# A list-scheduled attention and feed-forward kernel: landings as measured, and new positions and engines for its jobs

## The chip, the cores and the metric

One Trainium2 chip, one of its cores. The metric is device time in microseconds (us), the median of runs. PE is TensorE (PEld its weight loads), DVE is VectorE, ACT is ScalarE, POOL is GpSimd and SP is SyncE, which here only starts transfers.

## The reference, cut to what matters

```python
k_proj = einsum('ks,bhsd->bhkd', E, k)          # 8 batches, 8 heads, 1024 tokens, 64 wide; k = 64
v_proj = einsum('ks,bhsd->bhkd', F, v)
scores = q @ k_proj.T / sqrt(64)                # 1024 x 64 per head
scores = scores - max(scores)                   # along the 64
attn   = exp(scores);  attn = attn / (sum(attn) + 1e-9)
x      = (attn @ v_proj) as 8192 tokens x 512
out    = (sigmoid(x @ w_gate) * (x @ w_val)) @ w_out      # 512 -> 1536 -> 512
```

## The kernel before, in words

**Work.** Each batch's tokens are taken as two blocks of 512, each from two halves (`hf` 0 and 1) of q; there are 16 blocks. Attention makes x for a batch, transposed, in `xT` (two buffers, by batch). Heads go in two groups of four, R = 0 and 1. For a block, three quads, each a third of the hidden width for gate and for value, are made by a scheme of seven products of half blocks (`seven`, `product`) in place of eight: it needs sums of weights (`tG`, `tV`, from `w_sum`, L557), sums of x (`xS`, from `xs_sum`, L557; the first, S1, is A21 + A22) and copies and sums of results (L542 on ACT, L1156 on DVE). The gate is a tanh on ACT (L542), its product with the value is L1225 on DVE. The output products (`o_jobs`) use sums of hidden values (`hS`, POOL and DVE, L557) and of wO (L1259). Block 0 and the outputs of block 0 and the last block are made plainly: `plain_steps` (L1044), 12 slices of 128 columns, eight matmuls of 512 columns each, and L1066 on DVE.

**Batch 0** (`first_batch`, `FB`) is made by PE transposes, not by transfers: k is projected (`project0`), scaled and copied (`kpd`, L914 on DVE or L542 on ACT), turned (`kpD`, L886), q is turned (`qT`, L752 on DVE or L542), then scores, row maxima (L1645), subtraction (L1672 on DVE, or a matmul with `minus` and `top` on PE), exponential (L542), row sums (L989, L990), normalisation (L996 on DVE or POOL, into `wT`, which holds nothing else yet), a turn into `eT`, the product with v (`h_xo`), copies into `xT` (L886 or L542). For the other batches the turns are transposing transfers that SP issues (L1493 for q, L1687 for the exponentials, L1751 for x), and the loads of a batch are issued by POOL (L569) once x of the batch before has been turned.

**Order.** No order is written by hand. Every piece of work is a job with an engine, a position, a cost and a release time. The `Scheduler` goes through time: each engine, when free, takes the ready job with the lowest position, if its buffers are to be had (8 PSUM banks, 13 buffers) and its position lies within `window` of PE's first open job. The result is each engine's fixed order; on the chip each waits on semaphores in that order. Positions are numbers in `AT` (all batches) and `FB` (batch 0); names with `f_` in `FB`, and `s0` to `s7`, `x1` to `x4`, `g1` to `g4`, `d0` to `d2` in `AT` choose an engine. `x1=1` puts the sum S1 of every block from 2 on (`x_sums`) on POOL. `EXTRA` adds time to jobs of a name: short visits of PE between longer products had such additions (`sc0`, `sc`, `xo`). `K_AT`, `Q_AT`, `V_AT` and `LAND` are the release times of jobs that read loads of batch 0 and of weights; `busy0` says from when each engine is free (for POOL, the end of its issue of the loads). Where PE has nothing ready before a time `warm`, it takes a filler: two matmuls of 128 columns of the identity into bank 7 (`busy(2)`), which keeps that bank until then.

**Loads.** E and F from SP; all else from POOL, in the order k (four quarters) with the first half of q, v, wG and wV parts 0 (two halves), 3 and 1, the second half of q, parts 4, 2 and 5. This start is not scheduled (`start_loads`); wO and batch 1's loads are jobs.

Of the kernel before, what the change touches and what calls it, by code (L numbers as in the profile page):

```python
# [21 lines left out]


AT = dict(
    window=39.691, step=0.195, lag=0.031, ostep=0.461, tanh=24.746, hidden=-7.261, oa=0.642, ob=4.537,
    sums=0.006, late=-2.968, sc=2.958, scs=0.019, out=-6.538, outs=0.319, loads=18.861, gap=0.015, kv=10.106,
    tq=0.36, xa=0.682, xb=19.738, kv1=-4.582, vv1=11.125, wo=9.153, f_wo=0, qt1=-10.965, sc1=8.783,
    scs1=0.553, late1=-8.564, out1=-6.359, outs1=0.013, osum=18.731, loads2=-2.786, tq2=15.696, kv2=5.021,
    xa2=2.02, xb2=5.69, o0=8.301, o0s=1.088, xs1=-1.514, sc2=-4.038, end=3.656, pesub=8.049, s0=0, s1=0, s2=0,
    s3=0, s4=0, s5=0, s6=0, s7=0, o0p=1, o1p=0, o2p=0, o3p=1, x1=0, x2=0, x3=0, x4=0, g1=0, g2=0, g3=0, g4=1,  # L30
    d0=1, d1=0, d2=1, dsub=-4.028, dexp=-11.886, dinv=-7.839, ddiv=-2.87, dplus=-7.33, dsnap=7.354,
    dmerge=-9.93, dcopy=0.06, dturn=1.147, pdma=0.652, pact=0.017, pdve=0.019, ppool=0.074, lag0=1.549,
    lag1=1.843, lag2=-0.006, lag3=0.662, lag4=0.576, lag5=-0.336,
)
FB = dict(
    pk0=7.446, pk1=-8.728, tk0=5.506, tk1=4.235, tq00=13.818, tq01=0.999, sc00=-4.241, sc01=-3.946,
    tp00=1.262, tp01=6.936, pv0=-1.685, pv1=6.136, xo00=-7.862, xo01=-9.679, tq10=-22.633, tq11=3.073,
    sc10=-0.964, sc11=-4.904, tp10=0.8, tp11=-10.391, xo10=15.714, xo11=-2.829, wq0=15.106, wq1=11.887,
    wq2=19.985, dsum=-12.859, dnorm=10.025, m0=1.346, m1=8.435, m2=-10.899, m3=-4.159, m4=15.774, m5=5.879,
    ms=9.909, xs0=-16.282, ld1=19.781, lda=-7.826, f_pk00=1, f_pk01=0, f_pk10=1, f_pk11=0, f_tk0=1, f_tk1=1,  # L40
    f_pv00=1, f_pv01=0, f_pv10=0, f_pv11=0, f_s00=0, f_s01=1, f_s10=0, f_s11=1, f_n00=1, f_n01=0, f_n10=0,
    f_n11=0, f_tq000=1, f_tq001=1, f_tq010=0, f_tq011=1, f_tq100=0, f_tq101=1, f_tq110=1, f_tq111=1,
    f_tp000=1, f_tp001=0, f_tp010=1, f_tp011=1, f_tp100=0, f_tp101=1, f_tp110=0, f_tp111=0, f_xo000=1,
    f_xo001=0, f_xo010=0, f_xo011=1, f_xo100=1, f_xo101=1, f_xo110=0, f_xo111=1, f_dp=0, f_dx=1, f_dq=1,
    f_dk=0, f_w2=1, f_late=0, f_q1=0, f_q2=0, f_wsG0=0, f_wsG1=1, f_wsG2=0, f_wsV0=0, f_wsV1=0, f_wsV2=0,
    f_xs0=0, f_xs1=0, tx10=-12.089, tx11=4.878, f_tx100=1, f_tx101=0, f_tx110=1, f_tx111=0, late0=-10.759,
    f_ou100=0, f_ou101=0, f_ou102=0, f_ou103=0, f_ou110=0, f_ou111=1, f_ou112=1, f_ou113=1,
)


# [110 lines left out]
class Scheduler:  # L161
# [2 lines left out]
    HOP = {"PE": 0.205, "ACT": 0.035, "DVE": 0.035, "POOL": 0.06, "SP": 0.1}  # L164

    EXTRA = dict(
        qt=0.12, qt1=0.16, turnk=0.1, turnk0=0.1, tp=0.1, tx=0.1, tk=0.1, tq=0.1, bc0=0.8, den0=0.2, sc0=0.15, xo0=0.2, sc=0.03, xo=0.04,
        copyG=0.028, copyV=0.028, copyO=0.028, tanh=0.015, kd=0.1, vd=0.1,
    )

# [13 lines left out]
    def job(self, eng, pos, body, release=0.0, name=""):  # L184
        j = Job(eng, pos, body, release, name)
        self.jobs.append(j)
        self.now = j
        body()
        j.cost += self.EXTRA.get(name, 0.0)
        self.now = None  # L190
        return j
# [194 lines left out]
def bass_linformer_attn__then__ffn_glu_sigmoid_kernel(  # L386
# [20 lines left out]
    with contextlib.ExitStack() as es:  # L407
# [9 lines left out]
        def within(shape, dtype):  # L417
# [52 lines left out]
        NB = 11  # L470
# [3 lines left out]
        bank = [  # L474
            es.enter_context(nc.psum_tensor(n, [P, 512], FP32))
            for n in ("pF0", "pF1", "pF2", "pF3", "pA0", "pA1", "pA2", "pA3")
        ]

        plan = Plan()
        busy0 = {"PE": 8.3, "ACT": 8.4, "DVE": 7.0, "POOL": 18.3, "SP": 8.3}  # L480
        sched = Scheduler(range(8), range(2 + NB), 8.3, AT["window"], 38.0, busy0, 21.0)
        sched.free["bank"][7] = 21.2

        def add(eng, fn, r=(), w=(), x=(), dma=None, cost=0.0, nbytes=0, port=False):
            if sched.now is not None:
# [23 lines left out]
        def new_group():  # L509
            group[0] = []  # L510
# [212 lines left out]
        def busy(n):  # L723
            for _ in range(n):
                mm(7, bank[7][:, 0:P], ident[:, :], ident[:, :], ["ident"], n=P)
# [54 lines left out]
        def h_xo_keep(hf, R, g, bk, eng):  # L780
            o = xT[0][:, hf, g, 2 * R : 2 * R + 2, :]
            i = PB(bk)[:, :].rearrange("p (x c) -> p x c", x=2)
            copy(eng, o, i, [], [("xTt", 0, 2 * hf + g, R)], bk, 512)


        def first_batch():
            K_AT, Q_AT = ((9.15, 10.45), (13.0, 14.3)), ((11.75, 15.6), (30.05, 31.4))
            V_AT = ((18.2, 18.2), (19.5, 20.75))
            ENGS = ("ACT", "DVE", "POOL")

            def step(name, key, n, body, keep, release=0.0):
                new_group()
                b = new_bank(dirty=True)
                p = FB[f"{name}{key}"] + 0.003 * n
                bodies = body if isinstance(body, list) else [body]
                rel = release if isinstance(release, tuple) else (release,)
                for f, at_ in zip(bodies, rel):
                    job("PE", p, lambda f=f: f(b), release=at_, name=name)
                for m, f in enumerate(keep):
                    eng = ENGS[FB[f"f_{name}{key}" + ("" if name == "tk" else str(n * len(keep) + m))]]  # L800
                    job(eng, p, lambda f=f, eng=eng: f(b, eng), name=name + "k")
# [21 lines left out]
            for hf in range(2):  # L823
# [39 lines left out]
                for R in range(2):  # L863
                    if not hf:
                        keep = [lambda b, eng, R=R, g=g: keep_v0(R, b, g, eng) for g in range(2)]
                        step("pv", R, 0, [lambda b, R=R, th=th: project_v0(R, b, th) for th in range(2)], keep, V_AT[R])
                    new_group()
# [3 lines left out]
                    for g in range(2):  # L871
                        eng = ENGS[FB[f"f_xo{hf}{R}{g}"]]
                        job(eng, p, lambda R=R, g=g, hf=hf, b=bb[g], eng=eng: h_xo_keep(hf, R, g, b, eng), name="xok")
            for _ in range(120):
                j = Job("PE", 9e9, lambda: busy(2), 0.0, "fill")
                sched.now = j
                busy(2)
                sched.now = None
                j.deps = {}
                sched.fillers.append(j)  # L880
# [36 lines left out]
        def project_v0(R, bk, th):  # L917
            src = KV[1][:, :, :].rearrange("p h (t d) -> p t h d", t=NT)
            for t in range(4 * th, 4 * th + 4):
                for g in range(2):  # L920
                    mm(
                        bk,
                        PB(bk)[64 * g : 64 * g + 64, 0:256],
                        EFT[:, t, 64:128],
                        src[:, t, 4 * R : 4 * R + 4, :],
                        [("KVp", 1, R, th), ("KV", 1, R), ("EFT", t // 4)],
                        start=(t == 0),
                        stop=(t == NT - 1),
                        tp=(0, 64 * g),
                        n=256,  # L930
                        conc=2,
                        fill=0.005 + 0.094 * (t % 4 == 0 and g == 0),
                    )

        def keep_v0(R, bk, g, eng):
            gg, hh = slice(64 * g, 64 * g + 64), slice(4 * R, 4 * R + 4)
            i = PB(bk)[gg, 0:256].rearrange("p (h d) -> p h d", h=4)
            copy(eng, vpD[0][gg, hh, g, 0:DH], i, [], [("vpD", 0, g, R)], bk, 270 if eng == "ACT" else 380)
# [71 lines left out]
        def send_p0(t):  # L1010
# [8 lines left out]
            )  # L1019

        LAND = {
            "G": (21.3, 22.7, 27.4, 35.4, 24.7, 32.8, 38.1),
            "V": (22.0, 23.4, 28.7, 36.7, 26.0, 34.1, 39.4),
        }

        def landed(n, j):
# [767 lines left out]
        def load_o():  # L1794
# [7 lines left out]
            )  # L1802

        first_batch()
        plain_steps()
        for i, f in enumerate((lambda R: load_kv(0, k, 1, R), lambda R: load_q(1, R), lambda R: load_kv(1, v, 1, R))):
# [108 lines left out]
```

## Time and profile before

| | us |
|---|---|
| median of 3 runs | 525.74 (525.73 to 525.82) |
| the profiled execution | 525.35 |
| its span, first to last instruction | 523.6 |
| mean granted TensorE clock | 0.997 |
| first matmul / first plain matmul / first quad of block 2 | 5.54 / 27.09 / 99.61 |
| PE busy from 100 to 500 us | 399.97 |

Busy shares of the span: PE 97%, DVE 87%, ACT 71%, POOL 28%. A busy PE is one with matmuls in flight. Times in the timeline are the start and the length of a run of like instructions; the lengths of pipelined instructions overlap, so that costs are taken from start to start. Transfers started by POOL are short as instructions; their landing comes 5 to 30 us later and is read from the part on transfers.

### The profile page before, as it was taken

To read this page: it belongs to the slowest core of one execution; us is meant where nothing else is said; L and a number is where in the kernel's file an instruction comes from. 1 tells how busy PE (TensorE), PEld (TensorE's weight loads), DVE (VectorE), ACT (ScalarE), POOL (GpSimd) and SP (SyncE) were. 2 spreads that over 40 slices of the span, in tenths; PEclk is the share of its full clock that TensorE was granted. 3 is DMA by queue.
4 is the path that set the end of the run, shared out by engine and by line. 5 is a ranking of instruction groups with operands and counts; after the bars stand their busy time and mean duration, and the time that the engine had idled before them with its cause. 6 is when DMAs were issued, how large, how long until landed. Compare 5 with 4: busy or idle time off the path is not lost.

```text
span 523.6 us, 12301 instructions
## 1 busy us (share of the span) xinstructions
PE 510.3 (97%) x4787; PEld 428.8 (82%) x4792; DVE 457.3 (87%) x867; ACT 371.2 (71%) x711; POOL 147.5 (28%) x180
## 2 busy tenths in 40 slices
PE   5799999999999999999999999999999999999997
PEld 5544786888888888888888888888888888888885
DVE  5789999688999889997999889998899979998770
ACT  2335776688867788667976789667987679667852
POOL 9930002520336022520236003350225102420110
PEclk9989999999999999999999999999999999999999
DMA  9999914899378955599277983889557992632004
GB/s 163 197 199 207 181 41 92 213 181 161 70 173 129 223 80 107 135 192 227 40 114 158 212 146 62 182 140 223 82 102 132 200 213 42 139 63 81 3 1 162
DMA packets 140522, 71.59 MB, mean 137 GB/s; under 512 B 97200, under 2 KB 132272, under 8 KB 140464
## 3 DMA queue, kind: packets, MB, share of 16 engines
q0 software_dynamic: 35904, 29.89, 37.2%
q1 hardware_dynamic: 104560, 40.91, 37.0%
q8 instruction: 38, 0.62, 0.5%
q14 instruction: 20, 0.16, 0.1%
HBM read 60.29 MB, written 16.78 MB: 147 GB/s over the span
## 4 chain that ended last, share of the span: by engine, by line
PE 93%; DVE 4%; DMA 1%; ACT 0%; issue 0%; POOL 0%; SPq 0%; DVEq 0%
PE pA L528 47%; PE pF L528 46%; DVE hT L1066 1%; DMA EF<-in_F_dram 1%; DVE wT L996 1%; DVE inv L989 0%; DVE top L1645 0%; ACT spare L542 0%; DVE xT L886 0%; DVE wG L557 0%; DVE topf L1645 0%; POOL wT L996 0%; DVE tV L557 0%; DVE inv L990 0%; DVE pA L1672 0%
## 5 line engine op out<-in xcount | busy, mean ns | idle before, releaser
L542 ACT ACTIVATE spare<-pF 128x512 f32<-128x512 f32 (+2 forms) x164 | 92.4, 581 | 36.4 <-PE pF L528 30.6
L557 POOL TENSOR_TENSOR hT<-hT,hS 128x512 bf16<-128x512 bf16 x42 | 49.1, 1188 | 243.5 <-PE pA L528 141.8
L542 ACT ACTIVATE spare<-pA 128x512 f32<-128x512 f32 (+2 forms) x153 | 87.8, 584 | 32.8 <-PE pA L528 23.0
L1734 POOL TENSOR_TENSOR KVs<-spare,inv 128x384 bf16<-128x384 f32 (+1 forms) x51 | 37.0, 731 | 77.8 <-ACT spare L542 66.3
L542 ACT ACTIVATE spare<-spare 128x512 f32<-128x512 f32 x74 | 46.8, 637 | 4.6 <-DVE spare L1156 4.4
L1156 DVE TENSOR_TENSOR spare<-pA,spare 128x512 f32<-128x512 f32 x59 | 39.7, 677 | 7.6 <-ACT spare L542 4.5
L528 PE MATMUL pA<-wO,hT 128*128 128x256 bf16 (+1 forms) x334 | 45.6, 280 | 0.1
L1156 DVE TENSOR_TENSOR spare<-pF,spare 128x512 f32<-128x512 f32 x52 | 35.4, 682 | 9.4 <-ACT spare L542 5.6
L1225 DVE SCALAR_TENSOR_TENSOR hT<-spare,pF 128x512 bf16<-128x512 f32 x63 | 42.6, 677 | 0.5
L528 PE MATMUL pF<-wO,hT 128*128 128x256 bf16 (+1 forms) x273 | 41.4, 295 | 0.2
L1225 DVE SCALAR_TENSOR_TENSOR hT<-spare,pA 128x512 bf16<-128x512 f32 x51 | 34.4, 678 | 3.8 <-PE pA L528 2.9
L528 PEld LDWEIGHTS pA<-wO,hT 128*128 128x128 bf16 x336 | 32.5, 98 | 6.2
L528 PE MATMUL pF<-xT,wV 128*128 128x256 bf16 (+1 forms) x220 | 35.0, 282 | 0.0
L528 PE MATMUL pF<-xT,wG 128*128 128x256 bf16 (+1 forms) x208 | 34.6, 289 | 0.3 <-DVE xT L886 0.2
L528 PEld LDWEIGHTS pF<-wO,hT 128*128 128x128 bf16 x276 | 26.5, 98 | 8.5
L528 PE MATMUL pA<-xT,wV 128*128 128x256 bf16 (+1 forms) x188 | 32.0, 291 | 1.0 <-ACT spare L542 1.0
L528 PE MATMUL pA<-xT,wG 128*128 128x256 bf16 (+1 forms) x200 | 32.4, 284 | 0.0
L528 PE MATMUL pF<-xS,tV 128*128 128x256 bf16 x208 | 31.2, 272 | 0.0
L528 PE MATMUL pA<-xS,wG 128*128 128x256 bf16 x192 | 28.9, 273 | 0.0
L528 PE MATMUL pA<-xS,tG 128*128 128x256 bf16 x184 | 27.6, 273 | 0.0
L528 PE MATMUL pF<-xS,wV 128*128 128x256 bf16 x184 | 27.4, 273 | 0.0
L528 PE MATMUL pF<-xS,tG 128*128 128x256 bf16 x176 | 26.4, 273 | 0.0
(169 smaller groups left out, 1291.1 us busy)
## 6 DMA issues: line engine op xcount, KB each, us to landing
out_dram<-ost SPq DMA_DIRECT2D x63, 256.0 KB, 2.5
KVs<-in_v_dram POOLq DMA_DIRECT2D x15, 512.0 KB, 10.3
KVs<-in_k_dram POOLq DMA_DIRECT2D x14, 512.0 KB, 7.7
Qb<-in_q_dram POOLq DMA_DIRECT2D x14, 512.0 KB, 16.0
wO<-in_moe_w_out_dram POOLq DMA_DIRECT2D x1, 1536.0 KB, 26.1
wG<-in_moe_w_gate_dram POOLq DMA_DIRECT2D x5, 256.0 KB, 16.1
wV<-in_moe_w_val_dram POOLq DMA_DIRECT2D x5, 256.0 KB, 16.9
KVs<-in_k_dram POOLq DMA_DIRECT2D x4, 256.0 KB, 6.6
```

The lines of the kernel that those rows point to most:

```text
L528: lambda e: e.matmul(o, lhsT, rhs, **kw),
L542: lambda e: e.activation(o, i, func, scale=scale),
L557: fn = lambda e: e.tensor_tensor(o, a, b, op)
L996: fn = lambda e: e.tensor_tensor(o, x, i, ALU.mult)
L1066: lambda e: e.scalar_tensor_tensor(hT[0][:, m, :], BF(sg), 1.0, PB(bv)[:, :], ALU.add, ALU.mult),
L1156: lambda e: e.tensor_tensor(PB(b)[:, :] if stay else BF(s), PB(b)[:, :], BF(s), ALU.add),
L1225: lambda e: e.scalar_tensor_tensor(o, y.rearrange("p (j c) -> p j c", j=2), 1.0, x.rearrange("p (j c) -> p j c", j=2), ALU.add, ALU.mult,),
L1734: fn = lambda e: e.tensor_tensor(xto.rearrange("p (g h d) -> p h g d", g=2, h=H)[:, hh[0] : hh[1], :, :], o[:, :, 0:DH].rearrange("p (h g) ...
```

## The change

It replaces the numbers of `AT` and `FB` and the planner's assumptions; no function's work changes. The cut below has all of the latter, and the engine choices that move work.

```diff
 AT = dict(
-    window=39.691, step=0.195, ..., sc=2.958, ..., out=-6.538, ..., xa=0.682, xb=19.738, ..., wo=9.153, ...
-    ..., sc2=-4.038, end=3.656, ..., x1=0, ..., pdma=0.652, pact=0.017, pdve=0.019, ppool=0.074, ...
+    window=43.429, step=0.213, ..., sc=0.426, ..., out=-9.903, ..., xa=6.379, xb=25.171, ..., wo=20.6, ...
+    ..., sc2=-4.115, end=3.543, ..., x1=1, ..., pdma=0.759, pact=0.021, pdve=0.026, ppool=0.053, ...
 FB = dict(
-    ..., f_pk01=0, f_tk1=1, f_pv00=1, f_s00=0, f_s10=0, f_s11=1, f_n00=1, f_n11=0, f_wsG1=1, f_wsV0=0, ...
+    ..., f_pk01=1, f_tk1=0, f_pv00=0, f_s00=1, f_s10=1, f_s11=0, f_n00=0, f_n11=1, f_wsG1=0, f_wsV0=1, ...
@@ Scheduler
-        qt=0.12, ..., bc0=0.8, den0=0.2, sc0=0.15, xo0=0.2, sc=0.03, xo=0.04,
+        qt=0.12, ..., bc0=0.8, den0=0.2, xo0=0.2,
@@
-        busy0 = {"PE": 8.3, "ACT": 8.4, "DVE": 7.0, "POOL": 18.3, "SP": 8.3}
-        sched = Scheduler(range(8), range(2 + NB), 8.3, AT["window"], 38.0, busy0, 21.0)
-        sched.free["bank"][7] = 21.2
+        busy0 = {"PE": 7.35, "ACT": 8.2, "DVE": 7.7, "POOL": 19.7, "SP": 7.35}
+        sched = Scheduler(range(8), range(2 + NB), 7.35, AT["window"], 37.0, busy0, 25.0)
+        sched.free["bank"][7] = 25.2
@@ first_batch
-            K_AT, Q_AT = ((9.15, 10.45), (13.0, 14.3)), ((11.75, 15.6), (30.05, 31.4))
-            V_AT = ((18.2, 18.2), (19.5, 20.75))
+            K_AT, Q_AT = ((7.3, 8.5), (11.1, 12.45)), ((9.8, 13.85), (29.0, 30.3))
+            V_AT = ((16.35, 16.35), (18.4, 19.6))
@@
-            for _ in range(120):
+            for _ in range(170):
@@
-            "G": (21.3, 22.7, 27.4, 35.4, 24.7, 32.8, 38.1),
-            "V": (22.0, 23.4, 28.7, 36.7, 26.0, 34.1, 39.4),
+            "G": (20.3, 21.6, 26.3, 34.4, 23.65, 31.65, 37.1),
+            "V": (20.95, 22.35, 27.65, 35.75, 25.0, 33.15, 38.45),
```

What the built programs show of it: PE starts on k's first quarter right behind the transposes of E and F (16 fillers stood between); batch 0's first half has its subtractions on PE for both head groups (one before) and its normalisations on DVE (two of four were on POOL); POOL issues batch 1's v ahead of wO and the second half of its k behind q; S1 of 14 blocks is on POOL, that of blocks 2 and 3 ahead of batch 2's loads; the four weight sums on POOL are those of wV's first third (wG's second before). The number of fillers used falls from 96 to 86 matmuls.

More of the change, by code (lines that the diff above doesn't have):

```diff
@@ L24 @@
 AT = dict(
[L25 to L33, printed above, removed]
+    window=43.429, step=0.213, lag=0.011, ostep=0.464, tanh=21.597, hidden=-6.907, oa=0.549, ob=4.538,
+    sums=0.447, late=-1.505, sc=0.426, scs=0.02, out=-9.903, outs=0.016, loads=18.806, gap=0.012, kv=10.052,
@@ new lines @@
+    tq=0.487, xa=6.379, xb=25.171, kv1=-0.479, vv1=16.37, wo=20.6, f_wo=1, qt1=10.731, sc1=6.703, scs1=0.023,
+    late1=-8.42, out1=-5.011, outs1=0.053, osum=20.656, loads2=4.118, tq2=11.749, kv2=4.432, xa2=9.481,
+    xb2=-6.344, o0=6.554, o0s=0.102, xs1=-1.114, sc2=-4.115, end=3.543, pesub=13.162, s0=0, s1=0, s2=0, s3=0,
+    s4=0, s5=0, s6=0, s7=0, o0p=1, o1p=0, o2p=0, o3p=1, x1=1, x2=0, x3=0, x4=0, g1=0, g2=0, g3=0, g4=1, d0=1,
+    d1=0, d2=1, dsub=-5.317, dexp=-17.482, dinv=-6.2, ddiv=-5.811, dplus=-3.25, dsnap=6.491, dmerge=-11.783,
@@ L34 @@
+    dcopy=2.796, dturn=-1.745, pdma=0.759, pact=0.021, pdve=0.026, ppool=0.053, lag0=1.3, lag1=1.293,
+    lag2=-1.302, lag3=0.509, lag4=0.756, lag5=-0.457,
 )
 FB = dict(
[L36 to L44, printed above, removed]
@@ L45 @@
-    f_dk=0, f_w2=1, f_late=0, f_q1=0, f_q2=0, f_wsG0=0, f_wsG1=1, f_wsG2=0, f_wsV0=0, f_wsV1=0, f_wsV2=0,
-    f_xs0=0, f_xs1=0, tx10=-12.089, tx11=4.878, f_tx100=1, f_tx101=0, f_tx110=1, f_tx111=0, late0=-10.759,
-    f_ou100=0, f_ou101=0, f_ou102=0, f_ou103=0, f_ou110=0, f_ou111=1, f_ou112=1, f_ou113=1,
+    pk0=15.403, pk1=-16.99, tk0=8.488, tk1=-14.934, tq00=7.381, tq01=-9.651, sc00=-9.907, sc01=-24.495,
+    tp00=12.189, tp01=-0.744, pv0=9.411, pv1=-5.578, xo00=1.333, xo01=-16.402, tq10=-6.727, tq11=6.953,
@@ new lines @@
+    sc10=-9.441, sc11=-11.644, tp10=10.439, tp11=10.864, xo10=8.058, xo11=-10.078, wq0=13.384, wq1=9.184,
+    wq2=20.207, dsum=-20.382, dnorm=7.126, m0=-13.283, m1=8.591, m2=-17.12, m3=-4.892, m4=7.653, m5=17.37,
+    ms=4.645, xs0=-3.154, ld1=27.986, lda=-2.593, f_pk00=1, f_pk01=1, f_pk10=1, f_pk11=0, f_tk0=1, f_tk1=0,
+    f_pv00=0, f_pv01=0, f_pv10=0, f_pv11=0, f_s00=1, f_s01=1, f_s10=1, f_s11=0, f_n00=0, f_n01=0, f_n10=0,
+    f_n11=1, f_tq000=1, f_tq001=1, f_tq010=0, f_tq011=1, f_tq100=0, f_tq101=0, f_tq110=1, f_tq111=0,
@@ new lines @@
+    f_tp000=0, f_tp001=0, f_tp010=1, f_tp011=0, f_tp100=1, f_tp101=1, f_tp110=0, f_tp111=0, f_xo000=1,
+    f_xo001=0, f_xo010=0, f_xo011=1, f_xo100=1, f_xo101=0, f_xo110=0, f_xo111=0, f_dp=0, f_dx=1, f_dq=1,
+    f_dk=0, f_w2=1, f_late=0, f_q1=0, f_q2=0, f_wsG0=0, f_wsG1=0, f_wsG2=0, f_wsV0=1, f_wsV1=0, f_wsV2=0,
+    f_xs0=0, f_xs1=0, tx10=-21.46, tx11=-4.012, f_tx100=1, f_tx101=0, f_tx110=1, f_tx111=0, late0=-9.502,
+    f_ou100=0, f_ou101=1, f_ou102=0, f_ou103=0, f_ou110=1, f_ou111=1, f_ou112=0, f_ou113=0,
@@ L166 @@
     EXTRA = dict(
-        qt=0.12, qt1=0.16, turnk=0.1, turnk0=0.1, tp=0.1, tx=0.1, tk=0.1, tq=0.1, bc0=0.8, den0=0.2, sc0=0.15, xo0=0.2, sc=0.03, xo=0.04,
+        qt=0.12, qt1=0.16, turnk=0.1, turnk0=0.1, tp=0.1, tx=0.1, tk=0.1, tq=0.1, bc0=0.8, den0=0.2, xo0=0.2,
         copyG=0.028, copyV=0.028, copyO=0.028, tanh=0.015, kd=0.1, vd=0.1,
```

## The prediction

> **What bounds the kernel now.** I read the page's busy shares first, then the windows, the chain of waits, the timeline by engine and the landings of the loads.
>
> The page's first part says that TensorE is the bound:
>
> ```profile
> PE 510.3 (97%) x4787; PEld 428.8 (82%) x4792; DVE 457.3 (87%) x867; ACT 371.2 (71%) x711; POOL 147.5 (28%) x180
> ```
>
> PE lacks 13.3 us of the span of 523.6: 5.54 before its first matmul, 2.7 after its last, 5.05 between. The windows (us; then busy time of PE, PEld, DVE, ACT, POOL; granted clock; DMA share; GB/s) place the last part:
>
> ```profile
> 20.00:22.00 2.00, 0.47 (x8) 0.20 (x4) 1.01 (x2) 0.00 (x0) 1.87 (x2) 1.00 1.45 195
> ...
> 27.00:31.00 4.00, 3.96 (x20) 1.25 (x20) 3.00 (x9) 0.60 (x1) 0.00 (x0) 0.66 1.46 200
> ...
> 100.00:200.00 100.00, 99.97 (x956) 87.22 (x955) 91.02 (x165) 80.81 (x154) 25.34 (x29) 1.00 0.80 149
> ```
>
> The reader is to see that from 100 us on nothing can be won, and that the head loses in two ways: PE stands (20 to 22 us), and runs at a reduced clock (0.66 on average in 27 to 31 us, 0.50 in its worst slices). The chain of waits from 19 us (start, us, what) says why:
>
> ```profile
> 19.72 1.30 DVE top L1645 x2
> ...
> 21.06 1.05 POOL wT L996
> ...
> 22.15 0.40 PE pF L528 x4
> ...
> 24.35 0.66 DVE inv L989
> ...
> 27.09 1.01 PE pF L528 x2
> ```
>
> The normalisation `wT<-EF,inv` stands on GpSimd at 21.06, behind the issue of all weight loads (the last, wO, is issued at 19.72 and takes 1.21). Its sums were ready at 18.15 and 18.94. The last line is the first matmul of the plain blocks. And earlier PE spends time on fillers while data are there:
>
> ```profile
> 7.28 1.91 PE L528 MATMUL pA<-ident 128*128 128x128 bf16 x16
> 9.12 0.67 PE L528 MATMUL pF<-KVs,EFT 128*64 128x256 bf16 x8
> ```
>
> k's first quarter is issued at 1.37 and takes 5.5 to land, so 6.9; the matmuls that read it start at 9.12, behind 16 fillers.
>
> **What stays.** Counted by form, the two programs' PE instructions differ in fillers (96, then 86) and in subtractions on PE (4, then 6 of 512 columns, 0.22 each; both more lie before the first plain matmul). With start-to-start times of the timeline (0.216 us for 512 columns, 0.109 for 256, 0.056 for 128) the work from the first plain matmul to the first quad of block 2 is 68.9 us in both. Before, it took 99.61 - 27.09 = 72.5: the half clock cost 1.3 (27.09 to 30.50 holds work for 2.1), PE stood for 1.6 in all (0.99 at 37.6 us), 0.7 is small gaps. So the time is: start of the plain matmuls, plus fixed work, plus stalls.
>
> **What costs nothing by itself.** The landings, GpSimd's free time, the filler allowance (170) and the dropped allowances for short visits are figures of the plan: no load starts earlier by them, and no instruction takes longer. They act through the order alone, which I read from the built program.
>
> **The head, step by step.** The first 25 loads keep their order on GpSimd's queue, so I take their landings from the trace: q 9.6 and 13.6, k's last quarter 12.3, v 16.2, 18.2 and 19.4, wG part 0 at 20.05 and 21.45, wV part 0 at 20.75 and 22.15, part 3 at 23.45 and 24.8, q's second half 28.75 and 30.1, part 4 to 33.0, part 2 to 35.5.
> - k starts at 7.4 when the transposes of E and F end. Scores need k's copies (2 x 0.4), q (9.6), a transpose and a copy (0.4 each): 11.6 where they were at 13.64.
> - Row maxima to 13.1; two subtractions on PE (0.22) in place of two on DVE (0.60); exponentials (0.55) to 14.55; sums and normalisation on DVE (0.8 + 0.6) to 16.3 and 18.0, where GpSimd gave 22.1 and 23.95.
> - v at 16.2, then ACT's queue: four copies and two exponentials from 17.3 to 20.15. First product at 20.2, its copies to 21.7.
> - First plain matmul: 21.8. The weights would allow 20.8. **-5.3 us** (20.8 to 24.5: a few hand-offs 0.2 later each).
> - Behind it: second halves wait 0.55 for an xT copy that queues on DVE behind a weight sum waiting for wG part 3 (23.45), and part 2 costs 0.2: 0.75 of stalls for 1.6, **-0.85**.
> - Fillers run on to 22 us, so the half clock should go: **-1.3** (0 to -1.3).
>
> As the rows stand, the clock fell though PE never stood for more than 1.7 us in a row. [...]
>
> Outside this path, GpSimd gives up the four weight sums of one third of wG for those of wV and two early normalisations for two late ones; before, it stood idle from 40 to 53 us, so it can hold them. Its first q load then goes out near 29.5 (33.79 before), since the sums ahead of it wait for wV part 3 (24.8) and take 3 x 1.2.
>
> First quad of block 2: 92.2 instead of 99.6, **-7.45**. The covers hold: block 1 has its k by 61.5 (same bytes in the queue; PE wants it at 62.8); wO lands some 5.3 later, behind v (2 x 2.66), at 51, when DVE reaches its first sum at about 52; DVE's queue from the first row maximum (31) to block 2's sums adds up to 55.5, so 87 for 92.
>
> **What is late next.** Batch 2. Its chain before:
>
> ```profile
> 103.50 1.55 POOL L569 DMA_DIRECT2D KVs<-in_k_dram x2 [4.59 <-DMA xT<-KVs]
> ...
> 144.69 6.00 SPq L1751 DMA_TRANSPOSE xT<-KVs  x3
> ...
> 152.85 0.60 PE L528 MATMUL pF<-xT,wG 128*128 128x256 bf16 x4
> ```
>
> Loads start when batch 1's last transpose lands; xT is ready near 150; PE uses it at 152.85, nearly 3 us of slack. After the change PE is 7.45 earlier, but the loads only some 5.6: x sum 1 now stands on GpSimd in front of them (1.19 by the row of its like, L557 on POOL), and the last xT transpose queues on SP behind the output stores. And PE's order has the products of token tile 1 just before the quads: at 143.0, then copy 0.5, division 0.8, GpSimd's next 0.6, SP 1.3 and about 2 to land: 149.1. PE reaches the quads at 146.9. **+2.2** (0 to 4.5). Later batches have 8 us between products and quads. The rest of the body: 0 to 2, by its 0.13 us of idle before; I take **+0.3**. The tail has the same steps: 0.
>
> **Sum** against the profiled execution: -5.3 - 0.85 - 1.3 + 2.2 + 0.3 = -4.95; span 518.65, its own time 525.35 becomes 520.4. The median of the runs is 0.39 above it: **520.8**.
>
> **Rivals.**
> 1. The whole head gain stays (batch 2 finds its xT in time): 525.74 - 7.5 = 518.2. For it: transposes land 3.2 us after issue at the median, and the loads may start earlier. Against: the order above. Chance 0.20.
> 2. The head gives half: ACT's chain of six steps slips, or the clock halves again as PE waits at 20 to 24 us. First plain matmul at 24, clock unchanged: -3.1 - 0.85 + 1 (smaller wait at batch 2) = -3, 522.8; with the whole wait 524. Chance 0.17.
> 3. **Slower.** The first x sum of 14 blocks goes from DVE (0.41) to GpSimd (1.19). The two engines get in each other's way:
>
> ```profile
> 34.41 1.61 DVE L557 TENSOR_TENSOR wG<-wG 128x512 bf16<-128x512 bf16 x1
> 34.55 1.17 POOL L557 TENSOR_TENSOR tG<-wG 128x512 bf16<-128x512 bf16 x1
> ```
>
> 1.61 in place of 0.41, for one GpSimd sum beside it. DVE is 91% busy in the body. If each of 14 sums cost PE 0.85, that is 11.9: 525.74 - 4.95 + 11.9 = 532.7. It decides from 4.95/14 = 0.35 us a block. [...] Against the rival: xT of later batches lands some 8 us before the sum's first reader, and DVE loses 14 x 0.34 of work. Chance 0.08.
> 4. It does nothing that can be measured (within 0.2%, about what a measurement here tells from no change): landings are the plan's figures alone and move no load. But PE's order does change, and DVE takes over GpSimd's normalisation. Chance 0.05.
>
> The forecast has the other 0.50. Faster: 0.50 + 0.20 + 0.16 = 0.86; same 0.05; slower 0.09. The range for 8 in 10 leaves out rival 3 and the outer parts of 1 and 2: 517.6 to 524.4.
>
> **What would show it.** First plain matmul (`xT,wG` 128x512) at 21.8; clock 1.0 in 25 to 30 us; no PE idle at 20 to 22; first quad of block 2 at about 92; a PE wait for the xT transposes near 147 to 149; no PE wait for POOL's xS after 160. Wrong, if the plain matmuls start after 25, if PE waits more than 5 us at batch 2, or if PE's idle after 160 us passes 2.

## The result, and the profile after

The changed kernel takes **529.68 us** (median of 4 runs, 528.95 to 530.42) against 525.74 beside it; the ratio is 1.0081 with a 95% interval of 1.0058 to 1.0104. It is slower by 0.8%. The prediction was 520.8 with a range to 524.4.

The profiled run took 528.95, its span is 527.2. The page's first part (busy time of each engine):

```profile
PE 513.4 (97%) x4784; PEld 427.8 (81%) x4784; DVE 448.3 (85%) x845; ACT 374.6 (71%) x717; POOL 166.0 (31%) x194
```

PE is busy 3.1 us longer for nearly the same work (it has 10 fillers less and two subtractions more). The windows shown of before have the head mended now and the body broken:

```profile
20.00:22.00 2.00, 2.00 (x36) 1.40 (x32) 1.93 (x5) 1.95 (x5) 0.74 (x2) 1.00 1.44 194
27.00:31.00 4.00, 4.00 (x26) 2.07 (x25) 2.91 (x5) 1.91 (x5) 1.56 (x2) 1.00 1.45 196
100.00:200.00 100.00, 95.79 (x885) 80.83 (x883) 86.84 (x152) 74.03 (x141) 28.55 (x32) 0.98 0.75 135
```

PE no longer stands in 20 to 22 us and its clock is full in 27 to 31; but between 100 and 200 us, where it had lost 0.03 us, it stands for 4.2, and the mean clock there is 0.98. PE's timeline gives the stages:

```profile
23.52 0.59 PE L528 MATMUL pF<-xT,wG 128*128 128x512 bf16 x2
...
94.66 0.60 PE L528 MATMUL pF<-xT,wG 128*128 128x256 bf16 x4
...
157.10 0.60 PE L528 MATMUL pF<-xT,wG 128*128 128x256 bf16 x4
...
184.31 1.92 PE L528 MATMUL pA<-KVs,EFT 128*64 128x512 bf16 x16
```

These are the first plain matmul, the first quad of block 2, the first quad of block 4 (the first to read x of batch 2), and the projection of batch 3's k and v. At the second and the fourth the PE work still to come is the same in both programs, so they cut the time into stages that can be compared; the third is not such a mark (2 us of PE work have changed sides). Before, they were at 27.09, 99.61, 152.85 and 181.76. So the head gains 4.95, the stretch from 94.66 to 184.31 takes 89.65 in place of 82.15 and **loses 7.5**, and the rest loses 1.05: -4.95 + 7.5 + 1.05 = +3.6, which is 528.95 - 525.35.

Where the 7.5 lie, by windows of ten (columns as above: PE, PEld, DVE, ACT, POOL, clock, DMA), first in before:

```profile
120.00:130.00 10.00, 10.00 (x95) 8.45 (x92) 7.88 (x13) 8.56 (x16) 0.00 (x0) 1.00 0.95 165
130.00:140.00 10.00, 9.97 (x105) 8.47 (x103) 10.00 (x18) 8.53 (x17) 3.38 (x3) 1.00 0.28 54
140.00:150.00 10.00, 10.00 (x107) 9.03 (x106) 9.90 (x27) 9.46 (x21) 4.53 (x6) 1.00 0.63 108
150.00:160.00 10.00, 10.00 (x95) 8.92 (x93) 9.95 (x19) 5.61 (x12) 4.42 (x5) 1.00 0.56 159
```

then in the changed kernel:

```profile
120.00:130.00 10.00, 10.00 (x96) 8.98 (x95) 6.26 (x10) 8.72 (x17) 3.37 (x3) 1.00 0.56 110
130.00:140.00 10.00, 9.24 (x99) 8.01 (x97) 7.44 (x13) 8.49 (x18) 0.00 (x0) 1.00 0.25 48
140.00:150.00 10.00, 8.68 (x78) 6.99 (x78) 10.00 (x23) 5.09 (x10) 2.19 (x3) 1.00 0.78 150
150.00:160.00 10.00, 7.96 (x61) 5.92 (x62) 10.00 (x20) 4.85 (x10) 8.02 (x10) 0.83 0.59 121
```

DVE is idle for 6.3 us in the first 20 and then full for 20; PE stands for 4.1 in the 40, and its clock falls. A full DVE alone does not explain that: in before it is as full from 130 to 160 us, and PE does not stand. DVE's timeline says what it waited for in its idle time, the scores of batch 2 (idle time before, in brackets):

```profile
127.57 0.69 DVE L1645 TENSOR_REDUCE topf<-pA 128x8 f32<-128x512 f32 x1 [2.01 <-PE pA L528]
...
131.07 0.69 DVE L1645 TENSOR_REDUCE topf<-pA 128x8 f32<-128x512 f32 x1 [1.60 <-PE pA L528]
...
133.91 0.69 DVE L1645 TENSOR_REDUCE topf<-pA 128x8 f32<-128x512 f32 x1 [1.42 <-PE pA L528]
```

And PE's timeline shows where it paid: nine of the twelve products of batch 2 with v (`vpD,eT`) stand in one cluster from 147.67 to 152.9, and five of them show a wait (0.16 to 0.64 us) for a bank that ACT or DVE has to empty:

```profile
149.17 0.29 PE L528 MATMUL pF<-vpD,eT 128*128 128x130 bf16 x2 [0.56 <-ACT spare L542]
150.10 0.34 PE L528 MATMUL pF<-vpD,eT 128*128 128x130 bf16 x3 [0.64 <-DVE inv L1717]
...
152.28 0.34 PE L528 MATMUL pA<-vpD,eT 128*128 128x130 bf16 x3 [0.55 <-ACT spare L542]
...
154.02 2.32 PE L528 MATMUL pF<-wO,hT 128*128 128x256 bf16 x10 [0.89 <-DVE hT L1225]
```

The last line is ten matmuls of 256 columns that take 2.1 us from start to start in place of 1.1: half clock, which costs 1.3 us up to 157.10 (six more take 0.97 in place of 0.65). With 4.2 of standing that is 5.5 of the 7.5. The other 2.0 are not shown as idle time, because the length given for a matmul (0.27 us for 256 columns) runs 0.16 past the 0.109 after which the next one starts, and covers that much of every gap. Counted from start to start, PE's gaps come to 1.8 us between 136.79 and 141.55, at the last scores and the first products, and to 4.3 from 148.28 to 154.02; with the half clock's 1.3 that is 7.4 of the 7.5. In the cluster GpSimd is in the chain too: ACT's copy at 150.16 waited 1.04 us for a division there.

### The profile page after: what moved, and what is told of

It reads as the page before. It is cut to its first block, busy times and chain, and to the rows that moved or that the text cites. A ratio compares the mean times of both kernels' runs of the same rounds, so it can differ in the third digit from the quotient of the medians.

```text
span 527.2 us, 12327 instructions
## 1 busy us (share of the span) xinstructions
PE 513.4 (97%) x4784; PEld 427.8 (81%) x4784; DVE 448.3 (85%) x845; ACT 374.6 (71%) x717; POOL 166.0 (31%) x194
## 4 chain that ended last, share of the span: by engine, by line
PE 94%; DVE 4%; DMA 1%; ACT 0%; issue 0%; SPq 0%
PE pA L528 50%; PE pF L528 44%; DVE hT L1225 1%; DVE hS L557 1%; DMA EF<-in_F_dram 1%; DVE topf L1645 1%; DVE pA L1672 0%; DVE spare L1156 0%; DVE KVs L1734 0%; DVE ost L1414 0%; DVE pF L1672 0%; DVE inv L1717 0%; ACT ost L542 0%; DVE xS L557 0%; DVE pA L1156 0%
## 5 line engine op out<-in xcount | busy, mean ns | idle before, releaser
L528 PE MATMUL pA<-wO,hT 128*128 128x256 bf16 (+1 forms) x396 | 57.2, 289 | 0.2 <-ACT ost L542 0.2
L1734 POOL TENSOR_TENSOR KVs<-spare,inv 128x256 bf16<-128x256 f32 (+1 forms) x47 | 33.5, 720 | 64.2 <-ACT spare L542 39.3
L1156 DVE TENSOR_TENSOR spare<-pF,spare 128x512 f32<-128x512 f32 x60 | 40.8, 683 | 11.0 <-ACT spare L542 3.8
L528 PEld LDWEIGHTS pA<-wO,hT 128*128 128x128 bf16 x396 | 38.1, 98 | 10.4 <-ACT ost L542 0.4
L1225 DVE SCALAR_TENSOR_TENSOR hT<-spare,pF 128x512 bf16<-128x512 f32 x59 | 39.7, 679 | 2.2 <-PE pF L528 0.6
L1225 DVE SCALAR_TENSOR_TENSOR hT<-spare,pA 128x512 bf16<-128x512 f32 x55 | 37.1, 680 | 4.9 <-PE pA L528 2.2
L528 PE MATMUL pF<-wO,hT 128*128 128x256 bf16 (+1 forms) x216 | 31.4, 291 | 0.9 <-DVE hT L1225 0.9
L528 PE MATMUL pA<-wT,hS 128*128 128x256 bf16 x216 | 29.2, 273 | 0.3 <-DVE hS L557 0.3
L528 PE MATMUL pA<-xS,tV 128*128 128x256 bf16 x184 | 27.6, 273 | 0.0
L528 PE MATMUL pF<-xS,wG 128*128 128x256 bf16 x184 | 27.3, 273 | 0.1
```

The lines of the kernel that those rows point to most:

```text
L528: lambda e: e.matmul(o, lhsT, rhs, **kw),
L1156: lambda e: e.tensor_tensor(PB(b)[:, :] if stay else BF(s), PB(b)[:, :], BF(s), ALU.add),
L1225: lambda e: e.scalar_tensor_tensor(o, y.rearrange("p (j c) -> p j c", j=2), 1.0, x.rearrange("p (j c) -> p j c", j=2), ALU.add, ALU.mult,),
L1734: fn = lambda e: e.tensor_tensor(xto.rearrange("p (g h d) -> p h g d", g=2, h=H)[:, hh[0] : hh[1], :, :], o[:, :, 0:DH].rearrange("p (h g) ...
```

## The experiments

All kernels differ from the changed kernel or from before only by the lines shown. Every one is timed against before on its own chip. The stages are those above, taken from each run's own profile and given as differences from before's (99.61, then 181.76 - 99.61, then the rest of the span).

| run | median us | ratio to before (95%) | head | to batch 3's projection | rest |
|---|---|---|---|---|---|
| the change | 529.68 | 1.0081 (1.0058 to 1.0104) | -4.95 | +7.5 | +1.05 |
| 1: S1 on DVE | 524.54 | 1.000 (0.9989 to 1.001) | -4.45 | +2.06 | +2.0 |
| 2: S1 of block 3 later | 526.74 | 1.003 (1.0014 to 1.0046) | -4.43 | +5.07 | +1.15 |
| 3: no subtraction in batch 2 | 529.12 | 1.008 (1.0057 to 1.0102) | -4.58 | +8.67 | +0.8 |
| 4: before, fillers alone | 524.38 | 0.9987 (0.9975 to 0.9999) | -1.03 | 0.0 | 0.0 |
| 5: order of 1, S1 on GpSimd | 525.33 | 0.999 (0.998 to 0.9999) | -4.56 | +2.04 | +2.0 |
| 6: order of the change, S1 on DVE | 529.66 | 1.0085 (1.0053 to 1.0116) | -5.13 | +7.26 | +0.95 |
| 7: 1 with before's surcharges | 528.7 | 1.0055 (1.0037 to 1.0073) | -4.50 | +6.77 | +1.55 |
| 8: before, S1 on GpSimd | 532.7 | 1.0125 (1.009 to 1.0161) | -1.00 | +7.22 | 0.0 |
| **9: 7, loads after stores** | **522.43** | **0.994 (0.9925 to 0.9955)** | -4.87 | +0.51 | +1.65 |
| 10: 8, loads after stores | 526.63 | 1.0027 (1.0012 to 1.0042) | -1.00 | +0.61 | +0.4 |
| 11: before, landings alone | 529.64 | 1.0084 (1.0061 to 1.0106) | +3.34 | +2.99 | +0.05 |
| 12: before, no visits alone | 530.55 | 1.0095 (1.0071 to 1.0119) | +1.60 | +2.00 | +0.6 |
| 13: no reciprocals, divisions | 526.95 | 1.0027 (1.0015 to 1.0038) | -4.41 | +5.46 | +0.55 |
| 14: 13, no ACT copies | 527.38 | 1.0045 (1.0028 to 1.0062) | -4.72 | +6.33 | +0.5 |

### Runs 1 to 4: which part

Run 1, in the changed kernel:

```diff
-    ..., x1=1, ...
+    ..., x1=0, ...
```

> The changed kernel with S1 of blocks 2 to 15 back on DVE (x1=0); all else as changed, and the head's order is the same. Theory A (batch 2's loads wait on GpSimd behind the S1 sum of blocks 2 and 3, so its scores come late and then all at once to a DVE that has stood idle, and DVE ends the wait): loads issued 1 to 2 us earlier, scores spread from about 126 us, first quad of block 4 at 152 to 155 instead of 157.1, time 524 to 526.5. [...] Theory C (batch 2 is late for another reason, the order of the new positions): 528.5 to 530.

Measured 524.54, no slower than before: one number of the table makes the whole loss, though the head's gain is still given back. The first quad of block 4 is at 149.25. But Theory A's reason is not borne out: the loads of batch 2 start at 100.39, as late as with S1 on GpSimd (100.34). PE's scores, with the same loads, run at 126.92, 128.45, 129.54 and on to 133.28; in the changed kernel at 127.15, 130.65, 133.49 and on to 136.79. They come later there because they stand later in PE's order, behind quads.

Run 2, in the changed kernel, keeps all 14 sums on GpSimd and moves that of block 3 behind the loads:

```diff
-    ..., xb2=-6.344, ...
+    ..., xb2=5.69, ...
```

> The changed kernel with one position of before: xb2=5.69 instead of -6.344, so S1 of block 3 stays on GpSimd but goes behind the loads of batch 2; all 14 S1 sums stay on GpSimd. Theory A: loads about 1.2 us earlier, first quad of block 4 at 153 to 156, time 525.5 to 527.5. Theory B (cost of GpSimd's sums throughout): 528.5 to 530, no gain before 160 us beyond 0.5.

Measured 526.74. The first quad of block 4 is at 149.27, as in run 1, with the loads at 100.26. So one sum of about 1.2 us ahead of the loads in the plan is what makes the bad cluster; another stretch (150 to 170 us, where PE stands for 2.8) keeps 3 us of the loss.

Run 3 leaves the changed kernel's order as it is:

```diff
         def lower(b, t, y, bk):
...
+            if b == 2 and sched.now is None:
+                return
```

> The changed kernel in its own order with the eight subtractions of batch 2 on DVE (8 x about 0.6 us between 134 and 150 us) left out, so that the exponentials of that batch are taken without subtracting the maximum. If DVE bounds the stretch from 134 to 154 us (theory A), the first quad of block 4 comes 3 to 5 us earlier than 157.1, the clock stays at full speed in 150 to 160 us, and the time is 524.5 to 527. If the chain of transfers or the banks bound it, the first quad moves by less than 1 us and the time is 528.3 to 530.

Measured 529.12, first quad of block 4 at 157.47: 4.8 us of DVE work less (the eight stand between 128.8 and 143.3 in the changed kernel, two of them before 134), and nothing gained. That DVE's sum of work is the bound falls. DVE only stood longer, waiting in its own fixed order. Windows and PE's timeline of run 3:

```profile
130.00:140.00 10.00, 9.38 (x101) 8.28 (x99) 4.62 (x8) 8.38 (x17) 0.00 (x0) 1.00 0.22 43
140.00:150.00 10.00, 8.73 (x81) 7.13 (x78) 8.80 (x20) 5.35 (x11) 2.46 (x3) 1.00 0.76 153
```

```profile
147.74 0.34 PE L528 MATMUL pF<-vpD,eT 128*128 128x130 bf16 x3
...
154.09 1.25 PE L528 MATMUL pF<-wO,hT 128*128 128x256 bf16 x5 [0.87 <-DVE hT L1225]
```

DVE goes into the cluster without a backlog (at 148.12 it waits 0.32 us for PE's product), and the cluster runs as it did: from 147.74 in place of 147.67, and with the same wait at its end (0.87 for 0.89). So it is not work left over from the late scores that holds it.

Run 4, in before:

```diff
-        sched = Scheduler(range(8), range(2 + NB), 8.3, AT["window"], 38.0, busy0, 21.0)
-        sched.free["bank"][7] = 21.2
+        sched = Scheduler(range(8), range(2 + NB), 8.3, AT["window"], 38.0, busy0, 25.0)
+        sched.free["bank"][7] = 25.2
...
-            for _ in range(120):
+            for _ in range(170):
```

> The kernel before with the filler numbers of the change alone (fillers to 25 us instead of 21, 170 instead of 120, bank 7 held to 25.2); the order of the other work is the same. The prediction's term: the half clock of 27 to 31 us goes, 524.1 to 524.8, with the first plain matmul still at 27.1. [...] Third: the held bank delays the plain blocks: slower than 526.

Measured 524.38. The first plain matmuls keep their place, the clock is full. The windows of run 4:

```profile
24.00:26.00 2.00, 1.98 (x38) 1.64 (x36) 1.93 (x6) 1.26 (x4) 2.00 (x3) 1.00 1.45 196
26.00:28.00 2.00, 1.75 (x18) 0.90 (x15) 2.00 (x6) 0.60 (x1) 0.18 (x1) 1.00 1.45 198
```

and of before in the same stretch:

```profile
24.00:26.00 2.00, 0.94 (x15) 0.56 (x16) 1.93 (x6) 1.26 (x4) 2.00 (x3) 1.00 1.45 197
26.00:28.00 2.00, 1.76 (x11) 0.80 (x10) 2.00 (x6) 0.59 (x1) 0.18 (x1) 0.58 1.45 196
```

The fillers lift PE's busy time from 0.94 to 1.98 of the two microseconds before, and the granted clock behind it from 0.58 to 1.00. The first quad of block 2 comes 1.03 earlier. The median is 0.13% below before's, at the edge of what the measurement tells. Of the named parts tried alone (runs 4, 8, 11 and 12) it is the only one that doesn't lose.

### Runs 5 and 6: is it the sums' execution, or the order planned for them?

The order is made as in run 1 (run 5) or as in the changed kernel (run 6); only when the instructions are written out, S1 goes to the other engine. PE's order is not touched by it.

```diff
         def xs_sum(blk, n, eng):
+            if sched.now is None and n == 1 and blk > 1:
+                eng = "POOL" if eng == "DVE" else "DVE"
```

> The order that the scheduler makes for S1 on DVE (that of the run with x1=0), but the 14 S1 sums are executed on GpSimd, each at its place in time. PE's order is that of the x1=0 run, instruction by instruction. Theory P (GpSimd's sums cost little in themselves; with x1=1 the scheduler plans batch 2's loads later and so puts batch 2's scores and products late in PE's order): 524 to 526, first quad of block 4 at 149 to 151. [...]

> The other half of the cross: the order of the changed kernel (planned with S1 on GpSimd; PE's order the same, instruction by instruction), but the 14 S1 sums are executed on DVE. Theory P: 528 to 530, first quad of block 4 at 156 to 158, half clock near 154. [...]

Measured 525.33 and 529.66: theory P, on both sides, and against theory Q, by which the execution on GpSimd is what costs. Windows of run 5, then of run 6:

```profile
140.00:150.00 10.00, 8.99 (x94) 8.03 (x93) 9.68 (x24) 5.72 (x13) 6.72 (x9) 1.00 0.79 167
150.00:160.00 10.00, 9.40 (x83) 7.62 (x82) 8.98 (x17) 7.42 (x15) 6.57 (x7) 1.00 0.89 175
```

```profile
140.00:150.00 10.00, 8.59 (x79) 7.07 (x79) 10.00 (x23) 4.93 (x11) 2.35 (x3) 1.00 0.80 154
150.00:160.00 10.00, 8.06 (x63) 5.95 (x63) 9.36 (x21) 4.96 (x11) 7.03 (x8) 0.83 0.51 114
```

Run 6 executes all its sums on DVE, starts batch 2's loads 0.6 earlier than the changed kernel (99.75), and has the full loss with the half clock. Run 5 executes 14 sums on GpSimd and has the span of run 1 (523.1 against 523.2). The loss belongs to the order.

### Runs 7 to 10: a second way to lose at the same place

Run 7 is run 1 with four more numbers of before; run 8 is before with `x1=1`:

```diff
-    ..., x1=1, ..., pdma=0.759, pact=0.021, pdve=0.026, ppool=0.053, ...
+    ..., x1=0, ..., pdma=0.652, pact=0.017, pdve=0.019, ppool=0.074, ...
```

> The changed kernel with S1 on DVE and the scheduler's surcharges of before (pdma, pact, pdve, ppool), which place batch 2's transfers earlier in the plan. If the rest of the loss at batch 2 and in the body is the order too, this recovers part of it: 521.5 to 523.5. If it is not, 524 to 525.5.

> The kernel before with x1=1 alone, so that S1 of 14 blocks is on GpSimd and planned there; in that plan batch 2's loads keep their time. Theory P: 524.3 to 526 (no loss where the plan doesn't move batch 2). Theory Q and the prediction's third rival (each sum on GpSimd costs PE something): 527 or more.

Measured 528.7 and 532.7, both far from what was expected; theory P as I had put it (a loss only where the plan moves batch 2's loads) is too narrow. Both have one long wait. ACT's timeline of run 7:

```profile
158.78 0.60 ACT L542 ACTIVATE ost<-pA 128x512 f32<-128x512 f32 x1 [4.10 <-DMA out_dram<-ost]
```

ACT can't write its output tile, since the store of what lies in it has not landed; PE behind it stands for 3.86 us and then runs at a reduced clock (0.74 in 160 to 170). Of the four stores issued between 147.4 and 150.6, behind the transposes of x, the quickest landed in 2.3 us and the slowest in 8.1; GpSimd had begun to issue batch 3's loads at 149.81. In run 8 it is 8.7 us and a wait of 5.38. Runs 9 and 10 make these loads wait for the four stores' landing, and change nothing else:

```diff
         def store(blk, tt):
...
+                w=[("sent", tt)] if sched.now is None and not held else [],
...
         def load_kv(n, src, b, R, after=()):
+            if b == 3 and sched.now is None:
+                held.append(1)
+                after = list(after) + [("sent", tt) for tt in range(4)]
```

> The order of the run with S1 on DVE and the surcharges of before, unchanged; batch 3's loads alone wait until the four output stores issued just ahead of them have landed (2 to 3 us later than they started). Theory S: PE's one wait of 3.9 us at about 155 us comes from the last of these stores, which landed 8.1 us after its issue instead of 2.4 because the loads of batch 3 were issued beside it; ACT could not write its output tile. By S that wait and the half clock behind it go, 521.5 to 523.5. If the store is late for another reason, or the loads are needed so early that batch 3 waits: 526 to 530.

> The same edit in the kernel before with x1=1 (532.7 without the edit; PE waited 4.4 us for ACT's output tile, a store took 8.7 us to land). Theory S: 524.5 to 527. If S1 on GpSimd is the cause there: 530 or more.

Measured 522.43 and 526.63, 6.3 and 6.1 us less. ACT's write in run 9, with no wait for a store:

```profile
154.20 0.62 ACT L542 ACTIVATE ost<-pA 128x512 f32<-128x512 f32 x1
```

Stores take 2.0 to 2.4 us there, the loads start at 153.35 in place of 149.81, and batch 3 does not miss the 3.5 us (the rest of the span is +1.65 against +1.55). **Run 9 beats both kernels**: 0.6% faster than before. The changed kernel itself does not lose in this way: its stores go out between 145.77 and 149.65, its loads of batch 3 from 159.78.

### Runs 11 and 12: the other named parts alone

Run 11 is before with the change's lines for `busy0`, the scheduler's start, `K_AT`, `Q_AT`, `V_AT` and `LAND`; run 12 is before with the change's line of `EXTRA`:

```diff
-        qt=0.12, ..., bc0=0.8, den0=0.2, sc0=0.15, xo0=0.2, sc=0.03, xo=0.04,
+        qt=0.12, ..., bc0=0.8, den0=0.2, xo0=0.2,
```

> The kernel before with one named part of the change: its landings, busy times and start as measured (K_AT, Q_AT, V_AT, LAND, busy0, 7.35, 37), old tables, old fillers. Theory P (the order decides, and the positions were made for other landings): the first plain matmul 0.5 to 2 us earlier than 27.1, but a new order at batch 2 with a loss there; 525.5 to 530. Rival (better figures give a better order): 522 to 525.

> The kernel before with another named part alone: no allowance for visits (sc0, sc and xo dropped from EXTRA). Theory P: no gain of its own, since each PE instruction lasts as long; the order changes, and batch 2's place in it: 525 to 531. Rival (the allowance held PE's order back): 523.5 to 525.

Measured 529.64 and 530.55, each slower than before, run 11 at the head already (first plain matmul at 28.76, 1.7 us later than before where 0.5 to 2 earlier was expected; PE waits 1.70 for an xT copy of DVE ahead of it). Truer landings with positions made for other landings give a worse order here. The new tables with before's landings were not tried.

### Runs 13 and 14: what PE waits for in the cluster

In the changed kernel's order, for token tiles 1 to 3 of batch 2, run 13 leaves out the reciprocals and the divisions (run 14 `keep_o`, ACT's copies, too):

```diff
+        def off(b, t):
+            return b == 2 and t > 0 and sched.now is None
...
-            job("DVE", p + late + AT["dinv"] * (b > 0), lambda: invert(t, hh, bk), name="inv")
+            job("DVE", p + late + AT["dinv"] * (b > 0), lambda: None if off(b, t) else invert(t, hh, bk), name="inv")
...
-            job(eng, p + late + AT["ddiv"] * (b > 0), lambda: divide(b, t, hh, bk, sb), name="div")
+            job(eng, p + late + AT["ddiv"] * (b > 0), lambda: None if off(b, t) else divide(b, t, hh, bk, sb), name="div")
```

> The changed kernel in its own order, with the reciprocals and divisions of batch 2's token tiles 1 to 3 left out (nine small and nine larger instructions on DVE and GpSimd; x of these tiles stays what it was). Theory R: PE's nine late products (147.7 to 152.9 us) wait for their banks, which wait for DVE's reciprocal behind other work, and the half clock follows from these waits: PE's idle time in 148 to 155 us falls from 3.1 to under 1.5, the clock stays full, and the time is 525.5 to 527.5. Theory L (the products only stand late in PE's order, and what they wait for is the ACT copies or the hidden value): 528.3 to 530.

> As the run before, with ACT's copies of these products left out as well, so that nothing but PE holds their banks. Theory R or ACT's copies: PE's idle time in 148 to 155 us under 1, 524.5 to 527. If PE waits for DVE's hidden value of block 3 whatever becomes of the banks: idle time still 2 or more, 528 to 530.

Measured 526.95 and 527.38. In run 13 PE's idle time in 148 to 156 us falls from 3.1 to 2.2 only, but the clock stays full (1.00 from 130 to 170 us), and 2.7 us are won. In run 14 the products run without a wait, ending at 149.9 in place of 152.9; then PE waits in one piece for DVE's hidden value of block 3 (PE's timeline of run 14):

```profile
152.74 1.37 PE L528 MATMUL pF<-wO,hT 128*128 128x256 bf16 x10 [2.62 <-DVE hT L1225]
```

Neither theory holds alone. The banks and DVE's queue end close to each other (with the banks free the products end 3 us earlier, but the `wO,hT` matmuls start at 152.74 in place of 154.02, 1.3 us earlier), so that taking one away uncovers the other. What the two share is the place: the products stand in PE's order right before matmuls that need block 3's last hidden values, and ACT, DVE and GpSimd have the short steps of both to do in the same six microseconds. The loss of the stretch is still +5.46 in run 13 and +6.33 in run 14, part of it the 1.8 of gaps before 142 us, which these runs don't touch. That this place is what costs is read from the traces; no run moves the products alone.

## Why the prediction was wrong, point by point

- **The bound** (PE, nothing to win after 100 us): right.
- **Head, "-5.3", first plain matmul at 21.8**: 23.52, so -3.6. Two steps failed. "Scores ... 11.6" were at 12.95: DVE's copies of k, q and the turned k stand in a row from 10.62 to 12.67. And the second normalisation, "18.0", ended at 19.7, because two row maxima of the second half stand before it on DVE:

```profile
17.84 0.68 DVE L1645 TENSOR_REDUCE top<-pF 128x8 bf16<-128x512 f32 x1
18.44 0.68 DVE L1645 TENSOR_REDUCE top<-pA 128x8 bf16<-128x512 f32 x1
19.04 0.68 DVE L996 TENSOR_TENSOR wT<-EF,inv 128x512 bf16<-128x512 f32 x1
```

- **"-0.85" of stalls**: they went, but 0.9 of others came (0.22 at 83.25 and 0.69 at 91.56, PE for ACT): 71.1 us from the first plain matmul to the first quad of block 2 where 70.4 were forecast.
- **"-1.3" for the half clock**: right. The clock is full (1.00 in 27 to 31 us), and run 4 puts the term alone at 1.03.
- The head's sum is therefore -4.95 in place of -7.45, between the forecast and rival 2. By itself this would have left the time below before's.
- **Batch 2, "+2.2 (0 to 4.5)": this is the step that failed**; it is 7.5. The place was right, the mechanism was not. I followed the chain of transfers ("products of token tile 1 ... at 143.0", xT at 149.1) against PE's arrival, and asked only whether the last transpose lands in time. The last products before the quads ran at 152.28 and 152.62, and no wait of PE for an xT transpose appears at all. What the order had done was to put the products of the batch late and close together, so that PE itself was held by their banks and by DVE: 6.2 us of gaps from start to start, and 1.3 of half clock behind them. That the order does it, and not the engine that executes the sums, is shown (runs 5 and 6); which of its entries is to blame is read from the traces. I had the order before me and read from it the sequence just ahead of the quads, not how many short steps on other engines lie between two entries of PE. For run 1's order the same number would have been good (+2.06), but by luck: its waits there are for ACT (1.01 and 0.60), not for a transpose.
- **S1 on GpSimd ahead of the loads**: I priced it as 1.19 us of delay for the loads. On the chip it delays them by about half a microsecond (the loads lag 1.8 us behind PE, as forecast, but run 1 has 1.3 of that without S1 on GpSimd); its effect went through the plan, which run 2 shows for one sum and runs 5 and 6 for all.
- **Rest, "+0.3"**: +1.05. In run 1's order it is +2.0, some 0.40 in each batch (61.16 us from projection to projection, 60.76 before). What makes it is not traced.
- **Rival 3 (slower)** had the sign, not the cause: no run shows its 0.85 us a block. Run 5 executes 14 sums on GpSimd at no cost that can be measured, though DVE's sums run longer beside GpSimd's here as well (its x sum of 0.42 took 1.37 at 157.45 us in the changed kernel, beside GpSimd's hidden sums). What came true is the prediction's "wrong ... if PE waits more than 5 us at batch 2": 6.2 from start to start, though only 4.2 as idle time.

## What to carry to other kernels

A list scheduler's table is fitted to its assumptions: a truer landing, one allowance less or one sum on another engine makes a new order everywhere, and its worth is not in the sum of the parts. When an order is new, go through it for clusters: places where PE's next entries need several short steps of the others at once. And where a load's start and a store that frees a buffer can meet, order them: a wait of a few microseconds for loads with slack was worth 6 us here.

## What the runs showed of the hardware that I had not expected

**A store beside loads.** Of four 256 KB stores, the quickest landed 2.3 (run 7) and 2.5 us (run 8) after its issue, and the last, with loads of 512 KB issued beside it, 8.1 and 8.7; with the loads held back all took 2.0 to 2.7 (runs 9 and 10). What in the loads makes the delay, no run here shows.

**The clock at part duty.** In the changed kernel the clock halved behind a stretch in which PE never stood for as much as a microsecond. Its windows:

```profile
148.00:150.00 2.00, 0.91 (x10) 0.51 (x7) 2.00 (x8) 1.01 (x2) 0.75 (x1) 1.00 0.29 111
150.00:152.00 2.00, 1.14 (x11) 0.66 (x11) 2.00 (x8) 1.56 (x4) 1.40 (x3) 1.00 0.53 202
152.00:154.00 2.00, 0.84 (x7) 0.40 (x7) 2.00 (x8) 1.11 (x3) 1.73 (x4) 0.84 0.88 111
154.00:156.00 2.00, 1.98 (x10) 1.44 (x11) 2.00 (x4) 0.00 (x0) 1.53 (x2) 0.50 0.94 182
```

The longest stand there is 0.89 us, and the clock falls inside it, at about 153.4 (an estimate from the 0.68 granted in 153 to 154); PE was busy for 2.89 of the six microseconds from 148 to 154, 48%. In run 13, with 1.45, 0.99 and 1.63 busy of each 2 us there (68%), it stayed at 1.00; in run 14 it fell behind one stand of 2.62 us in one piece (0.94 in 152 to 154, 0.50 in 154 to 156). What decides it, these runs don't show.

**The half clock in some executions only.** Of 24 executions of before (beside runs 1 to 4) 12 took 524.3 to 524.5 us at a mean clock of 1.000, nine 525.5 to 525.8 at 0.997, and three 526.8 to 527.3 at 0.990 to 0.993. The profiled execution (525.35 at 0.997) has its half clock at 27 us, and it costs 1.3 us there; that the others at 0.997 have it at the same place is likely, not shown. That is why run 4's median stands only 0.6 under before's. Two of run 4's ten executions took 525.6 and 525.7 at 1.000, so something other than the clock can cost as much; what it is stays open.
